# Group 0's first q blocks in halves: three blocks instead of two, and a new order of issue

## The chip, the cores and the metric

The kernel runs on one core of one Trainium2 chip. The metric is the device time of one execution in microseconds (us). Three runs of the kernel before gave 236.28, 236.67 and 236.83 us; their median is 236.67 us.

## The reference

`x` has 2048 rows of 512 values (bf16). A small vector `c` gives six modulation vectors of 512, `silu(c) @ w_mod`: a shift, a scale and a gate for each of two stages.

```
h = layernorm(x) * (1 + ca) + sa
x = x + ga * attention(h)
h = layernorm(x) * (1 + cb) + sb
x = x + gb * (gelu(h @ w_gate) * (h @ w_up)) @ w_down
```

The attention has 32 heads of 16 values. Row s looks at 8 rows only: s, s-2, ..., s-14; rows before the first are masked. `q`, `k`, `v` come from `h @ wqkv`, the softmax goes over the 8 logits, and the result goes through `wo`. The inner width of the second stage is 1792.

## The kernel before, in words

**Groups.** The 2048 rows are four groups of 512, numbered 0 to 3, and a group is four chunks of 128 rows. For each group the kernel does:

1. a layernorm (statistics on VectorE at L430 or on ScalarE at L408 and L419, a root on POOL at L471, the normalisation on VectorE at L448);
2. a transpose, so that the 512 features lie on partitions. Group 0 is transposed on TensorE (L509) and group 1 too (L484); groups 2 and 3 by a DMA transpose that SP issues (L490);
3. scale and shift while the transposed tile is moved to the tile hT: group 0 by L543 (VectorE) and L545 (ScalarE) in half tiles of 256 rows, group 1 and 3 by L527 (ScalarE), group 2 by L525 (POOL);
4. twelve q, k and v blocks of four matmuls with 512 columns (L598), each copied out of PSUM by ScalarE (L618, L620, L624). For group 0 two q blocks are made in two halves of 256 columns (L580), so that they can begin when only the first half of hT is there;
5. logits: VectorE multiplies q with eight shifted copies of k (L664, four products of 2.29 us), TensorE sums over the 16 values of each head in groups of 32 columns (L678), softmax on VectorE and ScalarE (L695 to L722);
6. v goes to a scratch tensor in HBM (L635) and comes back as shifted copies, the tile V (L644); VectorE multiplies with the probabilities (L771, four products), TensorE sums (L790), ScalarE copies (L801);
7. the output projection (L811) and the addition to x (L820), a second layernorm, and the gated FFN: g and u blocks (L844), gelu and copies on ScalarE (L878, L885), their product on VectorE (L896), the down projection (L856, L868), the last addition (L903) and the store.

**The head.** Before group 0's data are there, TensorE runs filler matmuls on a zeroed tile (L217, 20 of them). The modulation columns for the first layernorm are 32 one-column matmuls in two groups (L348, the function `mods`), added up by VectorE (L355); the evictions L543 and L545 need them.

**Order.** The work is written as 135 generators, each yielding its steps in order (`Op`: the engine, an estimated length, the steps it comes after, the slots it takes and gives). The list ORDER holds one generator number for each step; steps are emitted in that order, and each engine runs its own steps in the order of emission. SP's list is the order of its DMA issues. Waits between engines come from semaphores on the data and on the buffers.

**Buffers that matter here.** PSUM has eight banks: four with the tag "mm" (filler, q, k, v, g, u, y), two with "att" (transposes, o, x1), and one tile of two banks, "lg" (logits; at the end also two o blocks). The tile hT has two buffers, so group 2's transpose must wait for the last q, k, v block of group 0. V has one buffer. Names used below: "q block j" is the j-th of the four q blocks; "visit" is a stay of TensorE with the 32-column groups of L678, L790 and L736 between wide matmuls.

**Group 0's transposes before.** `transp0` makes two steps of eight transposes. The first half's go to the two "att" banks, the second half's to two "mm" banks. PART tells which engine evicts which of the four feature tiles: VectorE two of the first half and three of the second, ScalarE two and one. `qkv_halves` then emits eight steps of two matmuls, first half and then second half.

Of the kernel before, what the change touches and what calls it, by code (L numbers as in the profile page):

```python
# [8 lines left out]
ACT = mybir.ActivationFunctionType  # L9
# [97 lines left out]
def kernel(  # L107
# [13 lines left out]
    nc = tc.nc  # L121
# [204 lines left out]
    def mods():  # L326
# [15 lines left out]
        for b in (1, 0):  # L342
            def f(b=b):
                if b:
                    B["mp01"] = T("mm", [P, 8], F32, "modT_ps")
                for ch in range(4):
                    for kt in range(4):
                        nc.tensor.matmul(B["mp01"][:, 4 * b + ch:4 * b + ch + 1],  # L348
                                         lhsT=B["wm01"][:, b, kt, ch * P:(ch + 1) * P], rhs=scT[:, kt:kt + 1],
                                         start=(kt == 0), stop=(kt == 3))  # L350
            yield Op("PE", 0.43, f, after=[f"wm{b}", "scT", "w15"], take=[SL["mm"]] if b else [],
                     give=[] if b else [SL["prod"]], fire=f"mp{b}")
# [141 lines left out]
    PART = ((0, (0, 1), False), (0, (2, 3), True), (1, (0,), False), (1, (1, 2, 3), True))  # L494

# [3 lines left out]

    def transp0(key, ev):  # L500
        for half in range(2):
            def f(half=half):
                for hf, dts, onv in PART:
                    if hf == half:
                        ps = T("mm", [P, len(dts), 256], BF16, "hTp") if half else T("att", [P, 2, SG], BF16, "hTp")
                        B[key, half, onv] = ps
                        for n, dt in enumerate(dts):
                            for c4 in range(2):
                                nc.tensor.transpose(ps[:, n, c4 * P:(c4 + 1) * P],  # L509
                                                    B[key][:, 2 * half + c4, dt * P:(dt + 1) * P], ident[:])  # L510
            yield Op("PE", 0.445, f, after=[f"{ev}.x{2 * half + 1}", "ident"], take=[SL["mm" if half else "att"]] * 2,
                     give=[SL["xn"]] if half else [], fire=f"{ev}.th{half}")
# [20 lines left out]
    def transp0_ev(key, dkey, sc, bi, ev, dep, eng):  # L533
        for half, dts, onv in PART:
            if onv != eng:
                continue
            for n, dt in enumerate(dts):
                def f(n=n, dt=dt, half=half, onv=onv):
                    if dkey not in B:
                        B[dkey] = T("hT", [P, CPS, DT, P], BF16, "hT")  # L540
                    o, i = B[dkey][:, 2 * half:2 * half + 2, dt, :], B[key, half, onv][:, n, 0:256].rearrange("p (c s) -> p c s", s=P)
                    if onv:
                        nc.vector.tensor_scalar(out=o, in0=i, scalar1=sc(dt), scalar2=bi(dt), op0=ALU.mult, op1=ALU.add)  # L543
                    else:
                        nc.scalar.activation(out=o, in_=i, func=ACT.Identity, scale=sc(dt), bias=bi(dt))  # L545
                yield Op("DVE" if onv else "ACT", 0.32 if onv else 0.455, f, after=[f"{ev}.th{half}"] + dep,
                         take=[SL["hT"]] if dt == 0 and half == 0 else [], give=[SL["mm" if half else "att"]] if n == len(dts) - 1 else [],
                         fire=f"{ev}.h{dt}.{half}")
# [22 lines left out]
    QKV0 = [(0, 0), (0, 1), (0, 2), (1, 0), (1, 1), (0, 3), (1, 2), (2, 0), (2, 1), (2, 2), (2, 3), (1, 3)]  # L571

    def qkv_halves():
        for half in range(2):
            for n, dt in enumerate(((2, 0, 3, 1), (0, 1, 2, 3))[half]):
                def f(half=half, n=n, dt=dt):
                    for j in range(2):
                        if half == 0 and n == 0:
                            B["qkvps", 0, 0, j] = T("mm", [P, SG], F32, "qkv_ps")
                        nc.tensor.matmul(B["qkvps", 0, 0, j][:, half * 256:half * 256 + 256],  # L580
                                         lhsT=wqkv[0][:, dt, j::4], rhs=B["hT", 0][:, 2 * half:2 * half + 2, dt, :],
                                         start=(n == 0), stop=(n == DT - 1))
                yield Op("PE", 0.218, f, after=[f"LN1.0.h{dt}.{half}", "wqkv0"],
                         take=[SL["mm"]] * 2 + [SL["q"]] if half == 0 and n == 0 else [], fire=f"qph.{half}.{dt}")
# [393 lines left out]
```

## Time and profile before

| | before |
|---|---|
| median of three runs | 236.67 us |
| lowest, highest | 236.28, 236.83 us |
| span of the profiled execution | 234.1 us |
| TensorE busy | 230.0 us, 1387 matmuls |
| VectorE busy | 170.4 us |
| ScalarE busy | 150.0 us |
| HBM read, written | 22.37 MB, 4.98 MB |

The profile is of one execution. Its span runs from the first to the last instruction, and the measured time of a run also has what lies before and after it, about 2.6 us here. A row of the timeline is: start in us, length in us, engine, line, operation, tiles written and read, shapes, count, and in brackets the idle time before it with what ended it. A row of the chain is: start, length, engine, tile, line, count. Matmuls are pipelined, and their ends are modelled: a matmul of 512 columns is shown with 0.38 us while the next one starts 0.22 us after it. So a start in the chain, which is the end of what stands before, lies about 0.16 us behind the start in the timeline.

### The profile page before, as it was taken

To read this page: it belongs to the slowest core of one execution; us is meant where nothing else is said; L and a number is where in the kernel's file an instruction comes from. 1 tells how busy PE (TensorE), PEld (TensorE's weight loads), DVE (VectorE), ACT (ScalarE), POOL (GpSimd) and SP (SyncE) were. 2 spreads that over 40 slices of the span, in tenths; PEclk is the share of its full clock that TensorE was granted. 3 is DMA by queue.
4 is the path that set the end of the run, shared out by engine and by line. 5 is a ranking of instruction groups with operands and counts; after the bars stand their busy time and mean duration, and the time that the engine had idled before them with its cause. 6 is when DMAs were issued, how large, how long until landed. Compare 5 with 4: busy or idle time off the path is not lost.

```text
span 234.1 us, 3675 instructions
## 1 busy us (share of the span) xinstructions
PE 230.0 (98%) x1387; PEld 108.2 (46%) x1387; DVE 170.4 (73%) x240; ACT 150.0 (64%) x283; POOL 18.6 (8%) x43
## 2 busy tenths in 40 slices
PE   7999999999999999999999999999999999999995
PEld 2755455434644444444444444444444444444443
DVE  3999999999997999999799788467747421222222
ACT  4899997976997758936656492546754343666400
POOL 2612461000100000100000010000001000000000
PEclk9999999999999999999999999999999999999999
DMA  6997989999969839553102963510000411000011
GB/s 218 373 364 213 202 213 171 276 391 303 176 152 236 291 92 200 98 114 103 56 0 57 202 109 60 156 56 0 0 4 0 90 45 45 3 0 0 0 48 45
DMA packets 36265, 30.21 MB, mean 129 GB/s; under 512 B 14872, under 2 KB 34328, under 8 KB 36248
## 3 DMA queue, kind: packets, MB, share of 16 engines
q1 hardware_dynamic: 35968, 29.72, 50.6%
q10 hardware_dynamic: 280, 0.26, 0.3%
q8 instruction: 11, 0.18, 0.3%
q14 instruction: 6, 0.05, 0.1%
HBM read 22.37 MB, written 4.98 MB: 117 GB/s over the span
## 4 chain that ended last, share of the span: by engine, by line
PE 98%; DVE 0%; issue 0%
PE g_ps L844 21%; PE u_ps L844 21%; PE y_ps L856 19%; PE qkv_ps L598 17%; PE x_ps L811 6%; PE o_ps L790 3%; PE LTp L678 3%; PE warm_ps L217 3%; PE y_ps L868 1%; PE qkv_ps L580 1%; PE hTp L484 1%; PE hTp L509 0%; PE modT_ps L305 0%; PE modT_ps L348 0%; PE gR_ps L369 0%; PE PTp L736 0%
## 5 line engine op out<-in xcount | busy, mean ns | idle before, releaser
L844 PE MATMUL g_ps<-h,Wg 128*128 128x512 bf16 x224 | 57.5, 379 | 0.0
L844 PE MATMUL u_ps<-h,Wu 128*128 128x512 bf16 x224 | 57.5, 379 | 0.0
L878 ACT ACTIVATE gl<-g_ps 128x512 bf16<-128x512 f32 x56 | 33.6, 600 | 24.8 <-PE g_ps L844 23.9
L856 PE MATMUL y_ps<-Wd,hht 128*128 128x512 bf16 x210 | 46.0, 379 | 0.0
L885 ACT CAST ub<-u_ps 128x512 bf16<-128x512 f32 x56 | 32.8, 586 | 18.3 <-PE u_ps L844 18.1
L598 PE MATMUL qkv_ps<-hT,wqkv 128*128 128x512 bf16 x184 | 42.1, 380 | 0.0
L896 DVE TENSOR_TENSOR hht<-gl,ub 128x512 bf16<-128x512 bf16 x56 | 23.0, 421 | 25.3 <-ACT ub L885 25.0
L664 DVE TENSOR_TENSOR pq<-qT,kT 128x4096 bf16<-128x4096 bf16 x16 | 36.3, 2292 | 0.0
L771 DVE TENSOR_TENSOR pv<-PT,V 128x4096 bf16<-128x4096 bf16 x16 | 36.0, 2286 | 0.0
L844 PEld LDWEIGHTS <-Wg 128*128 128x128 bf16 x224 | 21.5, 98 | 27.3 <-issue 2.1
L844 PEld LDWEIGHTS <-Wu 128*128 128x128 bf16 x224 | 21.8, 98 | 26.6 <-issue 0.4
L856 PEld LDWEIGHTS <-hht 128*128 128x128 bf16 x210 | 20.5, 98 | 24.8
L598 PEld LDWEIGHTS <-wqkv 128*128 128x128 bf16 x184 | 20.1, 114 | 19.7 <-issue 3.0
L903 DVE TENSOR_TENSOR ot<-y_ps,x 128x512 bf16<-128x512 f32 x15 | 10.3, 689 | 20.2 <-PE y_ps L856 17.2
L471 POOL TENSOR_TENSOR rstd<-rstd,neghalf 128x4 f32<-128x4 f32 (+1 forms) x9 | 8.8, 980 | 154.1 <-DVE rstd L460 85.5
L527 ACT ACTIVATE h<-h,modT,scl 128x512 bf16<-128x512 bf16 x12 | 8.8, 802 | 11.6 <-DMA h<-xn 11.6
L811 PE MATMUL x_ps<-woP,oT 128*128 128x512 bf16 x64 | 15.3, 379 | 0.0
L430 DVE BATCH_NORM_STATS2 st<-x 128x6 f32<-128x512 bf16 x19 | 12.9, 680 | 3.1 <-DMA x<-in_A_x_dram 2.9
L820 DVE TENSOR_TENSOR x<-x_ps,x 128x512 bf16<-128x512 f32 x16 | 10.8, 686 | 5.0 <-PE x_ps L811 5.0
L801 ACT CAST oT<-o_ps 128x512 bf16<-128x512 f32 x16 | 8.9, 592 | 2.7 <-PE o_ps L790 2.7
L618 ACT CAST qT<-qkv_ps 128x512 bf16<-128x512 f32 x16 | 9.2, 587 | 2.2 <-PE qkv_ps L598 2.1
L620 ACT CAST kT<-qkv_ps 128x512 bf16<-128x512 f32 x16 | 9.5, 596 | 1.2 <-PE qkv_ps L598 1.2
(85 smaller groups left out, 181.5 us busy)
## 6 DMA issues: line engine op xcount, KB each, us to landing
V<-vscr SPq DMA_DIRECT2D x12, 520.0 KB, 10.4
wm<-in_w_mod_dram SPq DMA_DIRECT2D x6, 512.0 KB, 5.4
vscr<-vT SPq DMA_DIRECT2D x4, 512.0 KB, 4.2
out_dram<-ot SPq DMA_DIRECT2D x15, 128.0 KB, 1.7
Wg<-in_B_w_gate_dram SPq DMA_DIRECT2D x1, 1792.0 KB, 11.0
Wu<-in_B_w_up_dram SPq DMA_DIRECT2D x1, 1792.0 KB
wqkv<-in_A_wqkv_dram SPq DMA_DIRECT2D x3, 512.0 KB, 8.3
x<-in_A_x_dram SPq DMA_DIRECT2D x3, 512.0 KB, 8.6
```

The source lines that it names most:

```text
L430: nc.vector.bn_stats(out=st[:], in_=src()[:, c4, :])
L598: nc.tensor.matmul(ps[:], lhsT=wqkv[blk][:, dt, j::4], rhs=B["hT", sg][:, :, dt, :], start=(dt == 0), stop=(dt == DT - 1))
L664: nc.vector.tensor_tensor(out=pq[:], in0=_ap(B["qT", sg][:, j, :], [[0, W], [1, SG]]), in1=_ap(kT[:, j, sg % 3 * SG + 2:sg % 3 * SG + 2 + ...
L771: nc.vector.tensor_tensor(out=t[:], in0=_ap(B["PT", sg][:, 0, :], [[SG, 2], [0, 4], [1, SG]]), in1=_ap(v[:, 0, j, :], [[8, 2], [4 * (SG + ...
L811: nc.tensor.matmul(ps[:], lhsT=B["oT", sg][:, j, c4::CPS] if sg else B["oT", sg][:, j, c4 * P:(c4 + 1) * P], rhs=woP[:, j, :], start=(j == ...
L820: nc.vector.tensor_tensor(out=x[:, c4, :], in0=B["x1ps", sg, c4][:], in1=x[:, c4, :], op=ALU.add)
L844: nc.tensor.matmul(ps[:], lhsT=Wt[:, dt, ft * P:(ft + 1) * P], rhs=B["h2T", sg][:, :, dt, :], start=(dt == 0), stop=(dt == DT - 1))
L856: nc.tensor.matmul(ps[:], lhsT=B["hh", sg, ft][:, c4 * P:(c4 + 1) * P], rhs=B["Wd", ft // 4][:, ft % 4, :], start=(ft == 0), stop=(ft == F ...
L878: nc.scalar.activation(out=gl[:], in_=B["g", sg, ft][:], func=ACT.Gelu_apprx_tanh)
L885: nc.scalar.copy(out=ub[:], in_=B["u", sg, ft][:])
L896: nc.vector.tensor_tensor(out=hh[:], in0=B["gl", sg, ft][:], in1=B["ub", sg, ft][:], op=ALU.mult)
L903: nc.vector.tensor_tensor(out=ot[:], in0=B["y", sg, c4][:], in1=B["x", sg][:, c4, :], op=ALU.add)
```

## The change

It does four things.

- **Three q blocks in halves.** The first half of group 0 is multiplied into three q blocks (twelve matmuls of 256 columns in four steps), and the second half then block by block (three steps of four matmuls). The fourth q block comes directly behind them, ahead of the first k block.
- **Transposes by chunk.** `transp0` makes four steps of four transposes, one for each chunk of 128 rows. The first half goes to the two "att" banks, the second half to the logits' tile (VectorE's three feature tiles) and one "mm" bank (ScalarE's one). Each bank is evicted by one engine: the table ONV takes the place of PART.
- **Less filler.** 17 filler matmuls instead of 20, and the first L348 group no longer has to come after the sixteenth of them; both L348 groups now stand ahead of all transposes.
- **A new ORDER.** SP's list of issues and POOL's list are the same as before, step for step. TensorE, VectorE and ScalarE have other orders over most of the program. The first differences behind the head: group 0's last k block moves from between group 1's two transposes to behind L369 and L305; the first logit product of group 0 moves behind group 1's normalisation; group 3's normalisation moves behind the softmax steps of group 0; some sums of L678 and L790 stand closer together; one logit product of group 2 moves ahead of group 1's V products.

The diff, without the list of numbers:

```
-            yield Op("PE", 0.43, f, after=[f"wm{b}", "scT", "w15"], take=[SL["mm"]] if b else [],
+            yield Op("PE", 0.43, f, after=[f"wm{b}", "scT"], take=[SL["mm"]] if b else [],
...
-    PART = ((0, (0, 1), False), (0, (2, 3), True), (1, (0,), False), (1, (1, 2, 3), True))
+    ONV = {(0, True): (0, 2), (0, False): (1, 3), (1, True): (0, 1, 2), (1, False): (3,)}
     def transp0(key, ev):
-        for half in range(2):
...
+        for c4 in range(CPS):
+            half, c = c4 // 2, c4 % 2
+            def f(c4=c4, half=half, c=c):
+                if c == 0:
+                    if half:
+                        B[key, 1, True] = T("lg", [P, 2, 2 * SG], BF16, "hTp")[:, 0, :]
+                        B[key, 1, False] = T("mm", [P, SG], BF16, "hTp")[:]
+                    else:
+                        B[key, 0, True] = T("att", [P, SG], BF16, "hTp")[:]
+                        B[key, 0, False] = T("att", [P, SG], BF16, "hTp")[:]
+                for onv in (True, False):
+                    for n, dt in enumerate(ONV[half, onv]):
+                        nc.tensor.transpose(B[key, half, onv][:, n * 256 + c * P:n * 256 + (c + 1) * P],
+                                            B[key][:, c4, dt * P:(dt + 1) * P], ident[:])
...
-    QKV0 = [(0, 0), (0, 1), (0, 2), (1, 0), (1, 1), (0, 3), (1, 2), (2, 0), (2, 1), (2, 2), (2, 3), (1, 3)]
+    QKV0 = [(0, 0), (0, 1), (0, 2), (0, 3), (1, 0), (1, 1), (1, 2), (2, 0), (2, 1), (2, 2), (2, 3), (1, 3)]
     def qkv_halves():
...
+        def mm(half, j, dt, n):
+            nc.tensor.matmul(B["qkvps", 0, 0, j][:, half * 256:half * 256 + 256], lhsT=wqkv[0][:, dt, j::4],
+                             rhs=B["hT", 0][:, 2 * half:2 * half + 2, dt, :], start=(n == 0), stop=(n == DT - 1))
+        for dt in range(DT):
+            def f(dt=dt):
+                for j in range(3):
+                    if dt == 0:
+                        B["qkvps", 0, 0, j] = T("mm", [P, SG], F32, "qkv_ps")
+                    mm(0, j, dt, dt)
+            yield Op("PE", 0.328, f, after=[f"LN1.0.h{dt}.0", "wqkv0"],
+                     take=[SL["mm"]] * 3 + [SL["q"]] if dt == 0 else [], fire=f"qph.{dt}")
+        for j in range(3):
+            def f(j=j):
+                for dt in range(DT):
+                    mm(1, j, dt, dt)
+            yield Op("PE", 0.437, f, after=[f"LN1.0.h{dt}.1" for dt in range(DT)], fire=f"qp.0.0.{j}")
...
-    pl.spawn(warmup(13, 20))
+    pl.spawn(warmup(13, 17))
```

More of the change, by code (lines that the diff above doesn't have):

```diff
@@ L492, in transp @@
             yield Op("SP", 1.65, f, after=[f"{ev}.x3"], take=[SL[dtag]], give=[SL["xn"]], fire=f"{ev}.t", lat=1.0)
-    PART = ((0, (0, 1), False), (0, (2, 3), True), (1, (0,), False), (1, (1, 2, 3), True))
     BY_PE = ('LN1.1', 'LN2.0')
     H_POOL = ('LN1.2',)
+    ONV = {(0, True): (0, 2), (0, False): (1, 3), (1, True): (0, 1, 2), (1, False): (3,)}
     def transp0(key, ev):
-        for half in range(2):
[L502 to L512, printed above, removed]
+        for c4 in range(CPS):
[12 more added lines that the diff above has]
+                                            B[key][:, c4, dt * P:(dt + 1) * P], ident[:])
+            yield Op("PE", 0.223, f, after=[f"{ev}.x{c4}", "ident"], take=[] if c else [SL["lg"], SL["mm"]] if half else [SL["att"]] * 2,
+                     give=[SL["xn"]] if c4 == 3 else [], fire=f"{ev}.th{c4}")
     def transp_ev(key, dkey, dtag, sc, bi, ev, dep):
@@ L533, in transp0_ev, with f @@
     def transp0_ev(key, dkey, sc, bi, ev, dep, eng):
[L534 to L538, printed above, removed]
+        for half in range(2):
+            for n, dt in enumerate(ONV[half, eng]):
+                def f(n=n, dt=dt, half=half):
                     if dkey not in B:
                         B[dkey] = T("hT", [P, CPS, DT, P], BF16, "hT")
-                    o, i = B[dkey][:, 2 * half:2 * half + 2, dt, :], B[key, half, onv][:, n, 0:256].rearrange("p (c s) -> p c s", s=P)
-                    if onv:
+                    o = B[dkey][:, 2 * half:2 * half + 2, dt, :]
+                    i = B[key, half, eng][:, n * 256:n * 256 + 256].rearrange("p (c s) -> p c s", s=P)
+                    if eng:
                         nc.vector.tensor_scalar(out=o, in0=i, scalar1=sc(dt), scalar2=bi(dt), op0=ALU.mult, op1=ALU.add)
@@ L545, in f @@
                         nc.scalar.activation(out=o, in_=i, func=ACT.Identity, scale=sc(dt), bias=bi(dt))
-                yield Op("DVE" if onv else "ACT", 0.32 if onv else 0.455, f, after=[f"{ev}.th{half}"] + dep,
-                         take=[SL["hT"]] if dt == 0 and half == 0 else [], give=[SL["mm" if half else "att"]] if n == len(dts) - 1 else [],
-                         fire=f"{ev}.h{dt}.{half}")
+                give = [] if dt != ONV[half, eng][-1] else [SL["att"]] if half == 0 else [SL["lg" if eng else "mm"]]
+                yield Op("DVE" if eng else "ACT", 0.32 if eng else 0.455, f, after=[f"{ev}.th{2 * half + 1}"] + dep,
+                         take=[SL["hT"]] if dt == 0 and half == 0 else [], give=give, fire=f"{ev}.h{dt}.{half}")
     stat = pool("stat_p", 4)
@@ L570 @@
     QKV = [(0, 0), (1, 0), (2, 0), (2, 1), (2, 2), (2, 3), (0, 1), (1, 1), (0, 2), (1, 2), (0, 3), (1, 3)]
-    QKV0 = [(0, 0), (0, 1), (0, 2), (1, 0), (1, 1), (0, 3), (1, 2), (2, 0), (2, 1), (2, 2), (2, 3), (1, 3)]
+    QKV0 = [(0, 0), (0, 1), (0, 2), (0, 3), (1, 0), (1, 1), (1, 2), (2, 0), (2, 1), (2, 2), (2, 3), (1, 3)]
     def qkv_halves():
[L574 to L584, printed above, removed]
-        for j in range(2):
-            pl.done[f"qp.0.0.{j}"] = pl.done["qph.1.3"]
+        def mm(half, j, dt, n):
[14 more added lines that the diff above has]
+            yield Op("PE", 0.437, f, after=[f"LN1.0.h{dt}.1" for dt in range(DT)], fire=f"qp.0.0.{j}")
     def qkv(sg):
@@ L591, in qkv @@
         for n, (blk, j) in enumerate(QKV if sg else QKV0):
-            if (sg, blk) == (0, 0) and j < 2:
+            if (sg, blk) == (0, 0) and j < 3:
                 continue
@@ L601, in qkv @@
             tk = {0: [SL["q"]], 1: [], 2: [SL["vs"]]}[blk] if j == 0 else []
-            yield Op("PE", 0.856, f, after=[f"LN1.{sg}.h{d}" for d in (("0.1", "1.0", "3.1") if sg == 0 else (2, 3))] + [f"wqkv{blk}"], take=[SL["mm"]] + tk,
+            yield Op("PE", 0.856, f, after=[f"LN1.{sg}.h{d}" for d in (("2.1", "3.1") if sg == 0 else (2, 3))] + ([f"wqkv{blk}"] if blk else []), take=[SL["mm"]] + tk,
                      give=[SL["hT"]] if last else [], fire=f"qp.{sg}.{blk}.{j}")
@@ L626, in qkv_ev @@
                      fire=f"qkv.{sg}.{blk}.{j}")
-        pl.done[f"qkv.{sg}.l"] = pl.done[f"qkv.{sg}.1.3"]
     def halo():
```

70 rows, old and new, of the table ORDER are left out of this document.

## The prediction

> **What bounds the kernel now.** I read the page first: busy time, then the chain that ended last.
>
> ```profile
> span 234.1 us, 3675 instructions
> PE 230.0 (98%) x1387; PEld 108.2 (46%) x1387; DVE 170.4 (73%) x240; ACT 150.0 (64%) x283; POOL 18.6 (8%) x43
> PEclk9999999999999999999999999999999999999999
> PE 98%; DVE 0%; issue 0%
> ```
>
> TensorE is 98% of the chain, so a change gains only what it takes out of TensorE's own row of work: filler, switching, or an idle gap. The share over the whole span hides VectorE (73%); the view by windows, cut to the attention part, shows it:
>
> ```profile
> 10.58:62.00 51.42, 51.42 (x378) 25.87 (x375) 50.80 (x65) 44.83 (x100) 10.34 (x8) 1.00 1.02 265
> ```
>
> From 10.58 to 62.00 us TensorE is busy 51.42 of 51.42 us, VectorE 50.80, and the DMA share is 1.02 (transfers overlap). Two engines and the DMA queue are full at once. What TensorE gains at the head, VectorE must gain too, or TensorE waits for it. Next, the chain in order of time:
>
> ```profile
> 1.25 4.88 PE warm_ps L217 x11
> ...
> 6.23 1.19 PE warm_ps L217 x5
> ...
> 9.43 0.65 PE warm_ps L217 x3
> 10.07 1.85 PE qkv_ps L580 x16
> ...
> 21.01 0.45 PE hTp L484 x8
> 21.45 0.34 PE gR_ps L369 x16
> 21.79 0.49 PE modT_ps L305 x16
> ```
>
> All the work that counts begins with the q blocks at 10.07; before it stand 20 filler matmuls (L217). The last view is the timeline between them.
>
> ```profile
> 8.20 0.54 PE L348 MATMUL modT_ps<-scT,wm 128*128 128x1 bf16 x16
> 8.34 0.41 DVE L448 TENSOR_SCALAR xn<-x,sums,rstd 128x512 bf16<-128x512 bf16 x1
> 8.78 0.17 DVE L355 TENSOR_TENSOR mod<-modT_ps,c 128x8 f32<-128x8 f32 x1
> 8.98 1.02 ACT L545 ACTIVATE hT<-hTp,mod 128x256 bf16<-128x256 bf16 x2 [0.82 <-DVE mod L355]
> 8.98 1.68 DVE L543 TENSOR_SCALAR hT<-hTp,mod 128x256 bf16<-128x256 bf16 x5
> ...
> 11.76 7.93 PE L598 MATMUL qkv_ps<-hT,wqkv 128*128 128x512 bf16 x36
> ```
>
> Five evictions in 1.68 us, one lasting 0.41, stand 0.32 apart; ScalarE's two in 1.02 last 0.56 and stand 0.46 apart. 36 matmuls of 512 columns in 7.77 us (7.93 less the pipeline's 0.16) are 0.216 each, so 0.108 for 256. Sixteen of those take 1.73, and 11.76 - 1.73 = 10.03 is the start that the q blocks would have had without a gap.
>
> **The head.** *The modulation columns.* The addition at 8.78 waits for the second L348 group (8.20 + 0.54 = 8.74). That group moves ahead of eight transposes (0.45 in the row of 21.01) and has one filler of 0.24 fewer before it, so it ends near 8.05 and costs nothing. Then VectorE's own queue binds: the last normalisation starts at 8.34, 0.32 later is 8.66. The addition starts 0.12 us earlier, the first eviction at 8.86; it ends at 9.27, and TensorE can start about 9.31. *TensorE by then:* the last four transposes wait for the chunk that ends at 8.75, take half of 0.45, and the one filler behind them 0.22: 9.25. Three fillers are gone; transposes in four steps are the same sixteen instructions. *Second half in time:* three blocks of the first half keep TensorE until 9.31 + 12 x 0.108 = 10.61. VectorE's last eviction ends at 8.98 + 1.68 - 0.12 = 10.54, ScalarE's third at 8.86 + 2 x 0.46 + 0.56 = 10.34, since L361 no longer stands ahead of it. No wait. The third block costs eight matmuls of 256 for four of 512: nothing. The logits' bank is unused so early, and three q tiles, the old warm-up and one transpose tile fit the four "mm" banks. Gain: 10.03 - 9.31 = **0.72 us**. Bounds: 0.4, if the second w_mod copy lands so late that L348 stays at 8.2 and the transposes follow it, and 0.8.
>
> **Fewer turns.** Each time TensorE goes from full-width matmuls to the 32-column groups (L678, L790, L736) and back, rows grow:
>
> ```profile
> 45.15 0.43 PE o_ps L790 x8
> ...
> 46.01 0.99 PE qkv_ps L598 x4
> ...
> 49.08 1.85 PE qkv_ps L598 x8
> ...
> 54.19 0.55 PE LTp L678 x8
> ...
> 84.22 1.01 PE o_ps L790 x16
> ```
>
> The first group of a visit takes 0.55 (54.19), one inside it 0.43; the first block after it 0.99 (46.01) where four matmuls are 0.86: 0.25 us a visit. The old list makes 15 visits, the new one 13; one of the two saved lies before 54 us, one behind. **0.25 us each.** Wanted by TensorE alone: 0.72 + 0.50 = 1.2 us less.
>
> **What VectorE gives back.** Its list up to the group 1 product that starts at 51.63 has the same instructions as before, and almost no idle time.
>
> ```profile
> 19.10 0.41 DVE L448 TENSOR_SCALAR xn<-x,sums,rstd 128x512 bf16<-128x512 bf16 x1
> 19.59 1.06 DVE L448 TENSOR_SCALAR xn<-x,mv,rstd 128x512 bf16<-128x512 bf16 x3
> 51.63 2.29 DVE L664 TENSOR_TENSOR pq<-qT,kT 128x4096 bf16<-128x4096 bf16 x1
> 53.83 1.28 DVE L820 TENSOR_TENSOR x<-x_ps,x 128x512 bf16<-128x512 f32 x2
> 56.16 0.68 DVE L820 TENSOR_TENSOR x<-x_ps,x 128x512 bf16<-128x512 f32 x1
> 56.88 0.69 DVE L430 BATCH_NORM_STATS2 st<-x 128x6 f32<-128x512 bf16 x1
> ```
>
> It starts 0.12 earlier. The step from 19.10 to 19.59 is 0.49 where 0.32 is normal: it waited for POOL's root, which now has a product of 2.2 us in front of it; 0.17 saved. So the product ends at 51.63 + 2.29 - 0.29 = 53.63. TensorE wants its group sums (54.19 in the chain, first matmul about 0.07 earlier) at 54.12 - 0.72 - 0.25 = 53.15 and gets them at 53.68: it waits 0.53 us, and 0.44 is left of the gain. Then VectorE saves 0.12 twice (56.16 to 56.88 is 0.72, where additions alone are 0.60 apart: another addition now stands between) and is not late for the next transposes. The second visit gives 0.25 more. In group 1's FFN stretch the next narrow place:
>
> ```profile
> 74.99 0.43 DVE L896 TENSOR_TENSOR hht<-gl,ub 128x512 bf16<-128x512 bf16 x1 [1.30 <-ACT ub L885]
> ...
> 80.07 4.49 DVE L771 TENSOR_TENSOR pv<-PT,V 128x4096 bf16<-128x4096 bf16 x2
> ```
>
> The last V product ends at 84.56. A 2.2 us product moves ahead of it, one 0.34 multiplication behind it, idle time (1.30 here, about 0.3 elsewhere) is used up, and 0.53 is brought along: 84.56 + 2.2 - 0.34 - 1.6 - 0.53 = 84.29, against what TensorE wants: the second half of the sixteen matmuls of 84.22 begins at 84.22 + 0.55, less the pipeline's 0.16, and 0.44 earlier: 84.17. About 0.1 lost, and perhaps 0.05 where two output tiles follow too closely for two banks. Sum: -0.72 - 0.50 + 0.53 + 0.15 = **-0.54 us**.
>
> **Transfers and queues.** SP's and POOL's lists are the same, so only the times of release change. ScalarE's list is reordered: L361 moves behind four q copies, its users L369 and the gate's copy stay ahead of their store on SP, which has to go at 25.3.
>
> ```profile
> 20.34 0.64 SPq L635 DMA_DIRECT2D vscr<-vT  x1
> 21.09 3.42 SPq L490 DMA_TRANSPOSE hT<-xn  x1
> ...
> 31.54 1.72 SPq L644 DMA_DIRECT2D V<-vscr  x2
> 37.46 3.46 SPq L490 DMA_TRANSPOSE hT<-xn  x1
> ```
> ```profile
> V<-vscr SPq DMA_DIRECT2D x1, 506.0 KB, 9.2
> ```
> ```profile
> 99.75 2.02 SPq L490 DMA_TRANSPOSE h<-xn  x1
> ```
> ```profile
> 41.68 2.29 DVE L771 TENSOR_TENSOR pv<-PT,V 128x4096 bf16<-128x4096 bf16 x1
> ```
> ```profile
> 43.39 0.82 ACT L527 ACTIVATE hT<-hT,mod 128x512 bf16<-128x512 bf16 x1
> ```
> ```profile
> 104.23 1.52 ACT L527 ACTIVATE h<-h,modT,scl 128x512 bf16<-128x512 bf16 x2 [2.36 <-DMA h<-xn]
> ```
>
> *Group 2's transpose* (21.09) takes the hT buffer that group 0's last k block reads. That block moves behind a transpose group (0.45 + 0.1), L369 (0.34) and L305 (0.49): it ends at 21.0 - 0.72 + 1.38, and the issue slips to 21.75, 0.65 late. Queued behind it on SP are the V copies; the last is issued at 32.2 and lands 9.2 later, 41.4. The first V product starts at 41.68 now and wants 41.39: no margin. Does 0.65 pass through? An issue lasted 3.42 and 3.46 with copies queued ahead, 2.02 with none, so I read its length as waiting for the queue: the v store ahead of it goes 0.2 earlier, and the issue ends when it did. Bounds: V lands between 0.2 earlier and 0.65 later; I take no shift. *Group 3's transpose* moves behind two softmax steps, 37.46 to about 39.2. The first L527 follows 5.9 us after the issue there (43.39) and needs no more than 4.5 after the one at 99.75 (104.23); so ScalarE starts its four between 43.7 and 45.1, and behind them in its queue, four L527 (two in 1.52: 0.71 apart) and 0.6 later stands the q copy that frees a bank: at 47.1 or 48.5. TensorE wants it for the block of 49.08, which moves ahead of one visit (0.55 + 0.13): 49.08 - 0.68 - 0.72 = 47.7. The 0.8 us of the worse case falls into the 0.53 that TensorE waits anyway, so 0 to 0.3; I take 0.
>
> **The clock.** At the start (rows of 1.25 and 6.23) 11 fillers take 4.88 us (0.44 each), later five take 1.19 (0.24): TensorE runs at half rate for about 5 us, though the granted clock of the page shows 9 throughout. [...]
>
> **Rivals.** *A, VectorE keeps up* (its long products take less when others move): no wait, 236.67 - 1.1 = 235.6. For it: the bare list leaves 0.6 us of VectorE's 51.42 idle. Against: part of that is the 0.17 counted already, the rest short gaps between dependent steps. Chance 0.14. *B, V lands late:* with the whole 0.65, the first V product starts at 42.1, 0.4 later than now; everything on VectorE follows, the group sums come 0.3 later than before, less 0.25 plus 0.15: +0.15, 236.8. From a landing 1.0 later it is slower than before by more than 0.4. For it: the hT buffer makes the transpose wait for certain. Against: the v store goes earlier, not later. Chance 0.28, a third of it beyond that point. [...] The thin stretch is shorter than now, so 0.06. *That the head gains nothing* (TensorE starts at 10.03 as now): the group sums are wanted at 53.87 and VectorE is there at 53.8, so no wait, -0.50 + 0.15: 236.3, inside the forecast; what the head gains is mostly waited away.
>
> **Numbers.** The sum is made on the profiled run, span 234.1; the runs' median is 236.67, so 2.6 us lie outside the span and stay: 236.67 - 0.54 = **236.1**. Forecast 0.52 (235.8 to 236.5), A 0.14, B 0.28, C 0.06. Range 235.5 to 237.1: it takes in A and most of B and leaves C out. A measurement of this kernel tells about 0.2% (0.47 us) from no change: faster below 236.20, slower above 237.14. Faster: 0.33 of the forecast's 0.52, and A: 0.47; slower: C and a third of B: 0.15; the same: 0.38.
>
> **What would show it.** Chain: L580 begins about 9.4 (ends are modelled) with 24 matmuls. Waits: TensorE's weight loads wait about 0.5 us for pq L664 near 53 us; without that, A. The transpose issue at 21.7 and the last V copy's landing: past 41.5 is B. 13 visits of L678 and L790 groups. I am wrong if VectorE's window from 10.5 on is no longer full, or if the V products begin after 41.7.

## The result and the profile after

The changed kernel takes **238.00 us** (median of five runs, 237.71 to 238.31); five runs of the kernel before beside it gave 236.59 (236.28 to 236.83). The ratio is 1.0055, with a 95% interval of 1.0041 to 1.0069: slower by 1.3 to 1.4 us (238.00 against the medians 236.67 and 236.59 of the kernel before), where 236.1 was predicted. Three of x1's ten runs below, its profiled one among them, had a granted clock of 0.993 and took 238.22 to 238.29 us, as had one of x3's (237.70) and one of x5's (239.21); the ratios take them in, and of x1's profile only rows of VectorE and POOL are read.

The page of the changed kernel, its span, busy time and chain:

```profile
span 235.7 us, 3655 instructions
...
PE 229.0 (97%) x1376; PEld 108.6 (46%) x1388; DVE 170.0 (72%) x240; ACT 150.5 (64%) x283; POOL 23.6 (10%) x43
...
PE 79%; DVE 10%; DMA 5%; POOL 3%; issue 1%; ACT 0%; DVEq 0%; POOLq 0%
```

TensorE held 98% of the chain and now holds 79%; VectorE, POOL and a transfer have moved in. (1376 of 1388 matmuls left a record, so the missing busy time is no reading.) One row stands out beside its old one: POOL, which does next to nothing in this kernel, is busy 23.6 us in place of 18.6. The two roots below make 4.0 of the 5.0; most of the rest is one instruction of L530, which comes up again further down. The chain in order of time says where it counts:

```profile
4.44 9.16 DMA x<-in_A_x_dram
17.43 3.32 POOL rstd L471
20.78 1.39 DVE xn L448 x4
...
66.65 0.86 PE g_ps L851 x4
...
100.92 2.93 POOL rstd L471
103.88 1.38 DVE xn L448 x4
```

Twice the chain runs through POOL's root of a layernorm (L471, 128 x 4 numbers), for 3.32 and 2.93 us. The first g block stood at 65.64 and now stands at 66.65, so 1.0 us is lost by then and 0.6 us later. (The chain's first row is the load of group 2's rows of x, which is followed at once by their statistics.) POOL's rows in the timeline, before and after:

```profile
13.49 1.02 POOL L471 TENSOR_TENSOR rstd<-rstd,neghalf 128x4 f32<-128x4 f32 x1 [3.12 <-DVE rstd L465]
18.30 1.25 POOL L471 TENSOR_TENSOR rstd<-rstd,neghalf 128x4 f32<-128x4 f32 x1 [3.79 <-DVE rstd L465]
...
96.08 1.01 POOL L471 TENSOR_TENSOR rstd<-rstd,neghalf 128x4 f32<-128x4 f32 x1 [35.42 <-DVE rstd L465]
```
```profile
13.75 1.03 POOL L471 TENSOR_TENSOR rstd<-rstd,neghalf 128x4 f32<-128x4 f32 x1 [3.37 <-DVE rstd L465]
17.43 3.31 POOL L471 TENSOR_TENSOR rstd<-rstd,neghalf 128x4 f32<-128x4 f32 x1 [2.65 <-DVE rstd L465]
...
100.92 2.92 POOL L471 TENSOR_TENSOR rstd<-rstd,neghalf 128x4 f32<-128x4 f32 x1 [39.39 <-DVE rstd L465]
```

The same instruction, on 128 x 4 numbers, takes 1.01 to 1.25 us everywhere else. What VectorE does at these two places, from the timeline after:

```profile
17.27 0.41 DVE L448 TENSOR_SCALAR xn<-x,sums,rstd 128x512 bf16<-128x512 bf16 x1
17.59 2.29 DVE L671 TENSOR_TENSOR pq<-qT,kT 128x4096 bf16<-128x4096 bf16 x1
20.78 1.06 DVE L448 TENSOR_SCALAR xn<-x,mv,rstd 128x512 bf16<-128x512 bf16 x3 [0.90 <-POOL rstd L471]
...
100.69 2.29 DVE L671 TENSOR_TENSOR pq<-qT,kT 128x4096 bf16<-128x4096 bf16 x1
103.88 1.38 DVE L448 TENSOR_SCALAR xn<-x,sums,rstd 128x512 bf16<-128x512 bf16 x4 [0.90 <-POOL rstd L471]
```

Both times the new order has put a logit product of 2.29 us on VectorE between the root's last input and the root's first user. The product ends at 17.59 + 2.29 = 19.88, the root at 17.43 + 3.31 = 20.74; the second time at 102.98 and 103.84. The root ends 0.86 us behind the product, nearly its whole length of 1.01: beside the product it has got nowhere. VectorE, which wants the root's result next, then stands idle for 0.90 us, twice. In the kernel before no root had a product beside it. What TensorE makes of it:

```profile
28.82 0.61 PE L685 MATMUL LTp<-pq,Mph 128*32 128x512 bf16 x8 [0.74 <-DVE pq L671]
...
112.08 0.62 PE L685 MATMUL LTp<-pq,Mph 128*32 128x512 bf16 x8 [0.53 <-DVE pq L671]
```

Theory: these two blocked roots are the loss. Rivals: the head costs something; the transfers of V or x are late; the new place of the sums costs.

### The profile page after: what moved, and what is told of

It is laid out like the page before. It is cut to its first block, busy times and chain, and to the rows that moved or that the text cites. A ratio compares the mean times of both kernels' runs of the same rounds, so it can differ in the third digit from the quotient of the medians.

```text
span 235.7 us, 3655 instructions
## 1 busy us (share of the span) xinstructions
PE 229.0 (97%) x1376; PEld 108.6 (46%) x1388; DVE 170.0 (72%) x240; ACT 150.5 (64%) x283; POOL 23.6 (10%) x43
## 4 chain that ended last, share of the span: by engine, by line
PE 79%; DVE 10%; DMA 5%; POOL 3%; issue 1%; ACT 0%; DVEq 0%; POOLq 0%
PE g_ps L851 21%; PE u_ps L851 21%; PE y_ps L863 14%; PE qkv_ps L606 11%; PE x_ps L818 6%; DMA x<-in_A_x_dram 5%; DVE pq L671 4%; PE o_ps L797 3%; POOL rstd L471 3%; PE LTp L685 2%; DVE xn L448 1%; PE y_ps L875 1%; DVE pv L778 1%; DVE st L430 1%; DVE e L729 1%
## 5 line engine op out<-in xcount | busy, mean ns | idle before, releaser
L606 PE MATMUL qkv_ps<-hT,wqkv 128*128 128x512 bf16 x180 | 41.0, 380 | 0.0
L606 PEld LDWEIGHTS <-wqkv 128*128 128x128 bf16 x180 | 19.6, 114 | 18.6 <-issue 2.3
L471 POOL TENSOR_TENSOR rstd<-rstd,neghalf 128x4 f32<-128x4 f32 (+1 forms) x9 | 12.8, 1427 | 149.0 <-DVE rstd L460 77.6
L532 ACT ACTIVATE h<-h,modT,scl 128x512 bf16<-128x512 bf16 x12 | 8.8, 805 | 20.3 <-DMA h<-xn 20.3
L408 ACT ACTIVATE gl<-x 128x512 bf16<-128x512 bf16 x13 | 8.3, 645 | 3.2 <-DVE x L827 2.9
L685 PE MATMUL LTp<-pq,Mph 128*32 128x512 bf16 x128 | 9.1, 382 | 1.3 <-DVE pq L671 1.3
## 6 DMA issues: line engine op xcount, KB each, us to landing
V<-vscr SPq DMA_DIRECT2D x12, 520.0 KB, 10.5
```

Source lines behind the costliest of these rows:

```text
L471: nc.gpsimd.tensor_tensor(out=k["rstd"][:, a:b], in0=k["rstd"][:, a:b], in1=neghalf[:, a:b], op=ALU.pow)
L606: nc.tensor.matmul(ps[:], lhsT=wqkv[blk][:, dt, j::4], rhs=B["hT", sg][:, :, dt, :], start=(dt == 0), stop=(dt == DT - 1))
L685: nc.tensor.matmul(B["LT", sg][H * g:H * g + H, 4 * t:4 * t + 4, :], lhsT=M[:], rhs=B["pq", sg, j][:, 4 * t:4 * t + 4, g * P:(g + 1) * P], ...
```

## The experiments

The median of the kernel before, run beside them, was 236.75 to 236.78 us, 0.17 above the 236.59 beside the changed kernel, so a difference between an experiment and 238.00 is uncertain by about as much; the ratios are to the kernel before in the same session. Where a list of numbers is edited, it is ORDER; x1, x2, x3 and x5 are edits of the changed kernel, x4, x7 and x9 of the kernel before, x6 of x3 and x8 of x6. For x5 and x7 ORDER was replaced as well, which is not printed; line numbers are two lower in the experiments' profiles (L469 is L471), and one higher in x8.

**x1, the first root away from the product.** Steps of ORDER between group 1's statistics and the first sums (L685) rearranged; VectorE's list there becomes: group 2's statistics, product, the two small inputs of the root (L460, L465), group 1's normalisation. On TensorE group 1's first transposes move behind the last v block, its second behind the last k block.

```
-    85, 59, 60, 60, 83, 60, 38, 83, 83, 85, 85, 37, 37, 37, 8, 37, 38, 38, 38, 38, 37, 38, 60, 61, 62, 37,
-    38, 11, 9, 12, 62, 61, 62, 24, 62, 25, 40, 109, 25, 37,
+    59, 83, 38, 40, 83, 83, 85, 85, 85, 60, 60, 60, 60, 37, 37, 37, 8, 37, 38, 38, 38, 38, 37, 38, 37, 38,
+    61, 62, 37, 11, 9, 12, 62, 61, 62, 24, 62, 25, 109, 25,
```

> The changed kernel, with group 0's first logit product (L671) put back ahead of the last two steps in front of group 2's root (L471), and group 1's transposes (L484) back behind the last v block. Theory (a root on POOL gets nowhere beside a logit product on VectorE): the root takes about 1.25 us again instead of 3.31, the normalisation behind it waits under 0.1 us instead of 0.90, VectorE's last group 1 product starts near 51.9 instead of 52.74, the first g block about 0.8 us earlier; time 237.2. The second such place (root at 100.92) stays as it is. Rival 1 (the loss comes from the head, where VectorE starts its statistics 0.26 us later, and from the order of TensorE's sums): VectorE only waits elsewhere, 237.8 to 238.1. Rival 2 (TensorE's transposes, now late, take the gain back): a wait of 0.4 us at L484 and 237.6.

Measured: 237.20 us, ratio to before 1.0030 (1.0014 to 1.0046). Rival 1 and rival 2 lie 0.6 and 0.4 off. The root, in the timeline:

```profile
19.88 1.25 POOL L469 TENSOR_TENSOR rstd<-rstd,neghalf 128x4 f32<-128x4 f32 x1 [3.97 <-DVE rstd L463]
```

It is 1.25 long again. The last product of group 1, expected near 51.9, starts at 53.11 in this profile; but VectorE's first statistics start at 11.97 there, and from them to that product it is 41.14 us, where it was 52.74 - 10.84 = 41.90. The first root is worth about 0.8 us. The edit also takes group 1's transposes and group 0's last k block back, so that x1 alone does not part the two; x4 does.

**x2, the second root away from the product.** Two steps change places: group 3's product goes ahead of the root, group 2's softmax subtraction beside it.

```
-    94, 75, 75, 118,
+    118, 75, 75, 94,
```

> The changed kernel, with the second place alone altered: group 3's second logit product now stands ahead of group 1's root (L471, at 100.92) and the softmax subtraction (L708, one operand in PSUM) behind it. Theory: beside that subtraction the root takes 1.0 us as it does elsewhere, not 2.92; VectorE's idle 0.90 at 103 is gone, TensorE's wait of 0.53 for the product at 112 too; time 237.5. Rival (TensorE waits there for VectorE because of its many long products, whatever the root does): the root is short, the wait stays, 237.9 to 238.1. If the root is as long beside the subtraction, the theory of a conflict with the product falls.

Measured: 237.41 us, ratio 1.0034 (1.0022 to 1.0047). Its timeline, POOL and VectorE:

```profile
102.73 1.01 POOL L469 TENSOR_TENSOR rstd<-rstd,neghalf 128x4 f32<-128x4 f32 x1 [40.46 <-DVE rstd L463]
```
```profile
102.49 1.23 DVE L706 TENSOR_TENSOR LTp<-LTp,mx 128x1024 f32<-128x1024 f32 x1
103.77 1.38 DVE L446 TENSOR_SCALAR xn<-x,sums,rstd 128x512 bf16<-128x512 bf16 x4
```

Beside a VectorE instruction that is as long as the root, but has one operand in PSUM, the root takes 1.01 and nobody waits. The wait at 112 is gone, and 0.59 us with it.

**x3, both edits.** The edits of x1 and of x2 together.

> The changed kernel with both alterations. Theory: the two losses are separate and add up, 238.0 - 0.8 - 0.5 = 236.7, level with the kernel before (236.6). Rival (the head and V's transfers cost as well): 237.2 or more.

Measured: 236.49 us, ratio 0.9995 (0.9983 to 1.0007): level with the kernel before. Together the two edits take 1.5 us off 238.00, which is the whole loss. Whether the rest of the change gains anything these runs can't tell; x7 does.

**x4, the kernel before with the first conflict alone.** In its ORDER group 0's first product (40) moves behind group 1's normalisation (60), and the last input of the root (85) ahead of the fourth normalisation.

```
-    40, 83, 83, 83, 85, 85, 85, 59, 37, 38, 5, 37, 37, 37, 38, 38, 38, 38, 37, 38, 60, 60, 60, 60,
+    83, 83, 83, 85, 85, 59, 37, 38, 5, 37, 37, 37, 38, 38, 38, 38, 37, 38, 60, 60, 60, 85, 60, 40,
```

> The kernel before, with one part of the change alone: group 0's first logit product (L664) behind group 1's normalisation, so that group 2's root (L471) runs beside it. Theory: the root takes over 3 us instead of 1.25, VectorE idles 0.8 to 0.9 us behind the product, all its later products are about 0.7 late, and the time is 236.6 + 0.7 = 237.3 (ratio 1.003). Rival (the place of this product does not matter, and the loss is made in the head or behind): 236.6.

Measured: 237.62 us, ratio 1.0041 (1.0029 to 1.0053), so 0.86 us from this one move. Its timeline:

```profile
17.78 3.31 POOL L469 TENSOR_TENSOR rstd<-rstd,neghalf 128x4 f32<-128x4 f32 x1 [2.65 <-DVE rstd L463]
```
```profile
17.94 2.28 DVE L662 TENSOR_TENSOR pq<-qT,kT 128x4096 bf16<-128x4096 bf16 x1
21.12 1.06 DVE L446 TENSOR_SCALAR xn<-x,mv,rstd 128x512 bf16<-128x512 bf16 x3 [0.90 <-POOL rstd L469]
```

The same 3.31 and the same 0.90, with nothing else of the change in the kernel.

**x5, the new head alone.** The change's ORDER up to the third q block, and from there the order of before on every engine.

```
-    QKV0 = [(0, 0), (0, 1), (0, 2), (0, 3), (1, 0), (1, 1), (1, 2), (2, 0), (2, 1), (2, 2), (2, 3), (1, 3)]
+    QKV0 = [(0, 0), (0, 1), (0, 2), (1, 0), (1, 1), (0, 3), (1, 2), (2, 0), (2, 1), (2, 2), (2, 3), (1, 3)]
```

> The change's head alone: transposes by chunk, three q blocks in halves, less filler, both modulation groups ahead of the transposes, and behind it the order of the kernel before on all engines. The prediction had the head at 0.72 us, of which VectorE lets 0.29 through: 236.3. What the traces say now: TensorE gains 0.2 (fourth block at 12.43, 12.63 before), and VectorE gains nothing, since its statistics wait for the second row block of x to land (10.8); then TensorE waits for VectorE as it does now and the time is 236.6 to 236.8. If the head is what costs: 237.2 or more.

Measured: 236.77 us, ratio 1.0005 (0.9985 to 1.0025). No gain or cost of the head shows; the interval is 0.2% wide to either side.

**x6, the head mended.** x3, with group 0's first two transpose steps (35), and the normalisations that they need (34), ahead of the second modulation group (22).

```
-    22, 33, 34, 34, 34, 34, 35, 35,
+    34, 34, 35, 35, 22, 33, 34, 34,
```

> The version with both roots moved, and in the head the first two transpose steps ahead of the second modulation group, so that they run while TensorE waits 0.58 us for that group's weights. If the late weights are what kept the evictions at 9.02: they start at 8.86, the q blocks at 9.3 instead of 9.8, TensorE gains 0.5. VectorE gains 0.16 at most, none if x's landing at 10.8 holds it. Time 236.3 (0.16 let through) to 236.5 (nothing); if TensorE's 0.5 counts in full, 236.0.

Measured: 236.45 us, ratio 0.9991 (0.9978 to 1.0004), as x3. In the timeline the q blocks begin at 9.75 and not at 9.3, and VectorE's statistics wait; the second fence is from the view of waits, between 7 and 13 us (PEld is TensorE's loading of weights):

```profile
9.75 2.81 PE L577 MATMUL qkv_ps<-hT,wqkv 128*128 128x256 bf16 x24
...
11.07 0.69 DVE L428 BATCH_NORM_STATS2 st<-x 128x6 f32<-128x512 bf16 x1 [0.31 <-DMA x<-in_A_x_dram]
```
```profile
PEld L577 <- DMA wqkv<-in_A_wqkv_dram: 0.4, 1, 0.4
```

The second modulation group came late once more (8.28), so that the evictions began at 9.07 and not at 8.86. Behind that the weights wqkv are the next thing awaited on TensorE, for 0.4 us, and x on VectorE. The expectation that TensorE gains 0.5 was wrong; that the time hardly moves was right.

**x7, the old head with x3's order behind it.**

```
-    QKV0 = [(0, 0), (0, 1), (0, 2), (1, 0), (1, 1), (0, 3), (1, 2), (2, 0), (2, 1), (2, 2), (2, 3), (1, 3)]
+    QKV0 = [(0, 0), (0, 1), (0, 2), (0, 3), (1, 0), (1, 1), (1, 2), (2, 0), (2, 1), (2, 2), (2, 3), (1, 3)]
```

> The head of the kernel before, and behind it the change's order with both roots moved: 13 visits in place of 15. By the prediction's 0.25 us a visit, with no gain of the head for VectorE to let through: 236.3 to 236.5. If the head is worth 0.2 in the whole, 0.2 above the version with both roots moved. If the visits are worth nothing, 236.7.

Measured: 236.33 us, ratio 0.9983 (0.9972 to 0.9993). This order beats both kernels, the one before by 0.4 us, and needs nothing of the new head's transposes, halves or filler.

**x8, x in two transfers.** x6, with group 1's rows of x loaded by two issues.

```
+        def halves():
+            yield Op("SP", 0.47, ldx(1, 0, 2), fire="x1a", lat=mb(0.25))
+            yield Op("SP", 0.47, ldx(1, 2, 4), fire="x1", lat=mb(0.25))
...
-            qs.append(one("SP", 0.55, ldx(g), fire=f"x{g}", lat=mb(0.5)))
+            qs.append(halves() if g == 1 else one("SP", 0.55, ldx(g), fire=f"x{g}", lat=mb(0.5)))
...
```

Not printed: the statistics of the first two chunks come after x1a alone, and ORDER has one more 6.

> The version with both roots moved and the head mended, and the second row block of x loaded by two transfers of half the size, one behind the other, so that VectorE's statistics of its first two chunks need the first transfer only. If that landing is what sets VectorE's start (idle 0.31 us there now, span less that start 223.13): the statistics begin about 0.35 earlier, directly behind the last eviction, and VectorE's list with them; TensorE has 0.1 to 0.2 us to spare there, so the time is 0.1 to 0.3 lower, 236.15 to 236.35. If the landing does not matter: 236.45. If the extra issue holds up the transfers behind it: 236.6 or more.

Measured: 236.34 us, ratio 0.9978 (0.9963 to 0.9993); 0.11 below x6, which these runs can't tell from nothing. VectorE, in the timeline:

```profile
10.66 0.68 DVE L431 BATCH_NORM_STATS2 st<-x 128x6 f32<-128x512 bf16 x1
...
13.70 0.70 DVE L431 BATCH_NORM_STATS2 st<-x 128x6 f32<-128x512 bf16 x1 [0.29 <-DMA x<-in_A_x_dram]
```

The statistics begin right behind the evictions, 0.41 earlier than in x6, and the next block of x (group 2's) takes 0.29 us of it back.

**x9, the kernel before with x late.** One issue moved: group 1's rows of x (6) behind the second block of wqkv (4).

```
-    6, 57, 57, 4,
+    4, 6, 57, 57,
```

> The kernel before, with one issue moved: the second row block of x behind the second block of wqkv (512 KB), so that it lands about 1.3 us later; nothing else. If VectorE's start on it sets the time of the whole (its list is full to 62 us): its statistics begin at 11.8 to 12.0 instead of 10.58, and the time is 1.2 to 1.4 us longer, 237.9 to 238.1. If what TensorE does at the head sets the time: the first q and k blocks are not later, and the time stays within 0.3 of 236.75.

Measured: 237.97 us, ratio 1.0053 (1.0033 to 1.0073). The row of VectorE's start:

```profile
12.30 0.69 DVE L428 BATCH_NORM_STATS2 st<-x 128x6 f32<-128x512 bf16 x1 [1.37 <-DMA x<-in_A_x_dram]
```

The start came later than the 11.8 to 12.0 that was expected; the time is as expected, 1.2 us longer. ScalarE's statistics of the same rows start at 12.30 too, so the run does not part the two engines. TensorE's q blocks began at 10.18, as they do with x in its old place in x7 (10.18) and x4 (10.15). So the end of this kernel hangs on when VectorE and ScalarE get these rows. Executions can be laid side by side by what follows that start (of VectorE's first statistics of group 1):

| kernel | start, us | span, us | span less start |
|---|---|---|---|
| before | 10.58 | 234.1 | 223.5 |
| x5, new head alone | 11.05 | 234.6 | 223.5 |
| after | 10.84 | 235.7 | 224.9 |
| x4, before with the first conflict | 11.19 | 235.5 | 224.3 |
| x2, after without the second conflict | 11.61 | 235.7 | 224.1 |
| x3, after without both | 10.77 | 233.9 | 223.1 |
| x6, x3 with the head mended | 11.07 | 234.2 | 223.1 |
| x7, x3's order, old head | 11.24 | 234.4 | 223.2 |
| x8, x6 with x in two transfers | 10.66 | 234.0 | 223.3 |
| x9, before with x late | 12.30 | 235.7 | 223.4 |

Without any edit to the transfers the start wanders by a microsecond. Each row is one execution; where the order behind the head is the same, what follows the start agrees to about 0.1 (before, x5, x9; x3, x6, x7), though the heads differ. From 223.5 the change's order gains 0.4 (x3, x6, x7) and its two conflicts cost 1.8 (the first 1.0, from x3 to x2; the second 0.8, from x2 to after), which makes 224.9. By the medians the two cost 1.5.

## Why the prediction was wrong

**The step that failed** is in "What VectorE gives back": the step from 19.10 to 19.59 "waited for POOL's root, which now has a product of 2.2 us in front of it; 0.17 saved". The product was taken as cover, 2.2 us in which the root would run to its end. They start 0.16 apart (17.43 and 17.59), and the root gets nowhere until the product has ended. In place of 0.17 saved, 0.82 was lost (0.90 idle, where 19.59 - 19.51 = 0.08 had been), which x1 and x4 show at 0.80 and 0.86 us of the whole. The second such place, group 1's root beside group 3's second product (at 108.69 before, 100.69 after), was missed altogether; that product is not among the moves that the list of the change names. x2 shows it at 0.59.

None of the roots in the trace of before has a product beside it, but another instruction on POOL has: the first of the four that scale and shift group 2 (L525). Merged, the four are one row of 6.05 us; one by one, with VectorE's products:

```profile
20.88 8.89 DVE L664 TENSOR_TENSOR pq<-qT,kT 128x4096 bf16<-128x4096 bf16 x4
...
26.62 3.80 POOL L525 TENSOR_SCALAR hT<-hT,mod 128x512 bf16<-128x512 bf16 x1 [7.07 <-ACT gl L408]
...
31.90 0.77 POOL L525 TENSOR_SCALAR hT<-hT,mod 128x512 bf16<-128x512 bf16 x1
```

The products end at 29.77, the first L525 at 30.42, 0.65 behind them; the other three take 0.77 each. (In the changed kernel the first takes 4.73, as L530.) So the price stood in this trace, on another line than the root's. That the root took 1.25 beside normalisations and 1.02 beside statistics was a second warning. From the first, the bound for the new overlap is the product's length and the root's, one behind the other. The roots agree with that: 0.86 us left to do behind a product of 2.29 (after), and 1.01 beside a subtraction that reads one operand from PSUM (x2). The pair of L525 and the product was not weighed, and it was the part of this trace that spoke against the change.

**The head (0.72 predicted).** TensorE got 0.2 in this profile and nothing in x5's, and no gain of time shows (x5). The rows of the timeline after:

```profile
8.07 0.55 PE L348 MATMUL modT_ps<-scT,wm 128*128 128x1 bf16 x16 [0.58 <-DMA wm<-in_w_mod_dram]
8.49 1.27 PE L514 MATMUL hTp<-ident,xn 128*128 128x128 bf16 x16
8.66 0.17 DVE L355 TENSOR_TENSOR mod<-modT_ps,c 128x8 f32<-128x8 f32 x1
...
9.02 1.77 DVE L547 TENSOR_SCALAR hT<-hTp,mod 128x256 bf16<-128x256 bf16 x5 [0.19 <-PE hTp L514]
...
9.81 2.78 PE L579 MATMUL qkv_ps<-hT,wqkv 128*128 128x256 bf16 x24
...
10.84 0.63 ACT L408 ACTIVATE gl<-x 128x512 bf16<-128x512 bf16 x1 [0.23 <-DMA x<-in_A_x_dram]
10.84 0.69 DVE L430 BATCH_NORM_STATS2 st<-x 128x6 f32<-128x512 bf16 x1
...
12.43 0.81 PE L606 MATMUL qkv_ps<-hT,wqkv 128*128 128x512 bf16 x3
```

The addition came at 8.66 as predicted. But the second modulation group waited 0.58 for its weights, and all transposes now stand behind it: the evictions began at 9.02 (8.86 predicted), the q blocks at 9.81 (9.31). The fourth block began at 12.43, where it had been 11.76 + 4 x 0.216 = 12.62; in x5 it began at 12.64. The stated bound "if the second w_mod copy lands so late" is this case, and its 0.4 was still too good. VectorE did not start 0.12 earlier but 0.26 later. Its evictions ended at 9.02 + 1.77 = 10.79, 0.13 behind those of before, and the rows of x came last: ScalarE waits for them until the same 10.84 (x6 and x9 show VectorE's own wait). So evictions done 0.12 earlier would have gained nothing. By x9 it is that start that counts.

**The visits (0.50).** Not contradicted: the timeline after has 13 visits, as counted, and the order without the conflicts gains 0.4 us with the old head and with the new (table), which would be 0.2 a visit. That this gain lies in the visits, and not in something else of that order, was not tried and stays open.

**VectorE as the bound.** Right, and the only reason why 0.9 us of idle there could cost that much. The last product of group 1 was to end at 53.63 and ended at 55.03. The difference of 1.40 is made of the start (0.26 + 0.12) and the root (0.82 + 0.17), to 0.03. The sign "if VectorE's window from 10.5 on is no longer full" came true: from 10.58 to 62.00 VectorE is busy 49.96 us, where it was 50.80. The wait of 0.53 for the product near 53 us does not show; TensorE waited earlier, 0.74 at 28.82 and 0.21 at 51.75.

```profile
42.80 8.90 DVE L778 TENSOR_TENSOR pv<-PT,V 128x4096 bf16<-128x4096 bf16 x4
51.60 1.23 DVE L391 TENSOR_TENSOR woP<-woP,gB 128x2048 bf16<-128x2048 bf16 x1
52.74 2.29 DVE L671 TENSOR_TENSOR pq<-qT,kT 128x4096 bf16<-128x4096 bf16 x1
```

**Transfers.** Right in what they cost. Group 2's transpose was issued at 22.23 (21.75 predicted) and lasted 1.68 in place of 3.42, so that it ended earlier than before, as it would if its length is waiting:

```profile
22.23 1.68 SPq L490 DMA_TRANSPOSE hT<-xn  x1
...
31.71 1.72 SPq L651 DMA_DIRECT2D V<-vscr  x2
```

The V products began past 41.7, which was to show that V is late; but they stand right behind the product that ends at 40.59 + 2.30 = 42.89, without idle time. VectorE was late, not V (the last copy, issued at 32.38, lands 8.6 later, at about 41.0), so that sign was badly chosen. Group 3's transpose was issued at 40.75 (39.2 predicted), and its four L532 began at 45.14, at the late end of 43.7 to 45.1; no wait of TensorE for the q copy behind them shows. Rival B did not happen, nor did A; nor did C, TensorE back at half rate at the q blocks for want of filler. That its rate falls when fillers are few is shown by no run: 24 matmuls of 256 columns took 2.62 us from 9.81 to 12.43, 0.109 each, and 2.62 as well in x3, with two fillers between 7.31 and 9.74. The place in group 1's FFN stretch where 0.15 was to be lost shows no wait: from 60 us on TensorE waits for VectorE once, at 112.08.

**The sum.** -0.54 was forecast. By the table the order gained 0.4, the head nothing, and the conflicts cost 1.0 and 0.8: +1.4, where 1.3 to 1.4 was measured. (The 2.6 us outside the span, which the forecast carries along, mix two executions: in the runs on record a time is 2.1 to 2.4 us above the span of the same run. The forecast is a difference from the median, so nothing hangs on it.)

The range left the result out because A and B were waits that the profile of before already had, grown or shrunk, and C was TensorE's rate. A new neighbour for an instruction on another engine was not looked for.

## What to carry to other kernels

When a step moves in one engine's list, write down what runs beside it on every other engine afterwards, and look in the old trace for the same pair of kinds of instruction, on whatever line, cut into single instructions: a merged row or a mean hides the one that was blocked. A small instruction on POOL whose result VectorE wants next is the one to look at; here it took its usual 1.01 us beside a VectorE instruction that reads PSUM (x2). Before pricing a gain at the start of a kernel, find the arrival that starts the busiest list: here putting off one block of x by 1.7 us in the profile made its span 1.6 us longer (x9), and no gain showed from the new head. Where two engines are full, lay executions side by side by the span that follows such a start; it showed 0.4 us where the times of single runs scatter by as much.

## What the runs showed of the hardware

- A root on POOL (128 x 4, f32) takes 1.01 to 1.03 us beside VectorE's statistics, maximum or a subtraction with a PSUM operand, 1.25 beside normalisations, and, beside a product of two bf16 operands in SBUF, until 0.86 to 0.87 us behind the product's end (after twice, x4 once). The product itself was not slowed (2.28 to 2.29).
- A scale and shift on POOL (128 x 512, bf16) takes 0.77 us beside instructions of VectorE that read PSUM, and 3.80 (before) or 4.73 (after) when it starts during the products. The group's four together take 4.88 us in x3 and 5.76 to 6.99 in before, after, x1, x2 and x4 to x7.
- In the first conflict and in x4 the root's record starts 0.16 us ahead of the product's (17.43 and 17.59; 17.78 and 17.94), and it was the root that was blocked: a root that starts a sixth of a microsecond earlier by the profile is not safe. Spans on POOL are rough by the page. Where POOL was 0.51 us ahead (L525 at 31.90, a product at 32.41 in before), the product took 2.40 us in place of 2.29.
- The arrival of the same transfer, behind the same list of issues, wandered between executions: ScalarE read group 1's rows of x without a wait at 10.54 in before and waited for them until 10.84 in after; VectorE waited for them until 11.07 in x6 and 11.24 in x7.
